# Weight remainders on one engine, and spread bit operations, in a three-part float32 kernel

## The chip, the cores and the metric

The kernel runs on one core of a Trainium2 chip. The metric is the device time of one execution in microseconds (us). The engines are PE (TensorE, matmuls), DVE (VectorE), ACT (ScalarE), POOL (GpSimd) and SP (SyncE, which here only issues transfers).

## What is computed

Three computations stand one behind the other; the last two matter here.

```python
def _attn_ref(q, k, v):        # 4 x 8 heads, 576 positions, 64 wide
    out_d = sm_attn(q_d, k_d, v_d)      # on means of 4 positions
    ...
    return (out_up + out_local)          # plus attention to the 7 nearest

def _moe_ref(x, w_gate, w1, w2):        # 2304 tokens of 512, 8 experts
    expert_idx = np.argmax(logits, axis=1)
    ...
        h = np.maximum(xe @ w1[e], 0.0)  # 512 -> 1024
        ye = h @ w2[e]                   # 1024 -> 512
        out[mask] = gate_w[mask, None] * ye

def _moe2_ref(x, w_in, w_out):          # 512 -> 2048 -> 512
    h = x @ w_in
    g = np.where(pos, h, np.where(neg, 0.0, (h + beta) ** 2 / (4.0 * beta)))
    return (g @ w_out)
```

w_in and w_out arrive as 64-bit floats; everything else is 32-bit.

## The kernel before

Every matmul operand is split into a rounded high part and a remainder, and three products are added: high by high, high by remainder, remainder by high. For a weight the high part (wh) is a cast on ACT (`wconv`, L169) and the remainder (wl) a subtraction (L170), which goes to POOL and DVE in turn. For the hidden tile of an expert the high part (hh) is made on ACT from PSUM (L890) and the remainder (hl) on DVE from PSUM and hh (L891). For an expert's inputs, xh and xl are made likewise from transposes (L893, L894).

The experts run one after another, sorted by their number of tokens, with 416, 360, 336, 312, 300, 288, 272 and 256 columns (CAPS). Expert e has eight steps f, here called slots; g = 8e + f counts them. In slot f TensorE first makes the hidden tile f + 1 (`emit_p1`, L942, twelve matmuls into s) and then takes hidden tile f into the output (`emit_p2`, L956, twelve matmuls into y: eight with hh, then four with hl). In slot 6 and slot 7 the transposes of the next expert's x stand in between, and in slot 7 the next expert's first hidden tile. Behind that, each slot issues weight conversions (`next_wt`: cast, remainder, and the load of the raw weight four places on, wraw, on SP's queue), at most two and only as far as seven buffers allow.

From slot g = CONV0 on, the first eight chunks of the 64-bit weights of the last network are also converted in the expert stage. A chunk goes through four stages: the load (`conv_load`, L815, craw, two buffers); `conv_guard`, a square on ACT (L846) and two operations on POOL (L847, L848); three bit operations on DVE (L834 to L836), which put a 32-bit float together; and the parts, a cast on ACT (L828) and a subtraction on POOL (L829). Each chunk takes four slots, and a chunk's stages lie several slots apart.

All instructions of an engine run in the order in which the code issues them. The rest of the program, the attention ahead of the experts (an order written out as a list) and the last network behind them (L999, L1089), is not touched.

Of the kernel before, what the change touches and what calls it, by code (L numbers as in the profile page):

```python
# [9 lines left out]
F32 = mybir.dt.float32  # L10
# [4 lines left out]
ALU = mybir.AluOpType  # L15
# [9 lines left out]
F2 = 2048  # L25
# [14 lines left out]
NWB, NWC, NWR = 3, 4, 4  # L40
NWT = NWB + NWC
NGR = 4
CONV0 = 16
PAT_MIN = float(np.array(0x38100000, np.uint32).view(np.float32))

C_ID = 0
# [67 lines left out]
def body(ctx: ExitStack, tc: tile.TileContext, qT, kT, kD, vS, vD, wg, w1, w2, w_in, w_out, cst, out, dbg=None, parts="all"):  # L114
    nc = tc.nc
    PE, ACT, DVE, POOL, SP = nc.tensor, nc.scalar, nc.vector, nc.gpsimd, nc.sync
# [11 lines left out]
    def bank(tag):  # L128
        return ps.tile([128, 512], F32, tag=tag, name=tag)
# [27 lines left out]
    wcount = [0]  # L157
# [6 lines left out]
    def wconv(raw):  # L164
        pool = wpools[wcount[0] % len(wpools)]
        wcount[0] += 1
        hi = pool.tile([128, 1024], F32R, tag="wh", name="wh")
        lo = pool.tile([128, 1024], F32R, tag="wl", name="wl")
        ACT.copy(out=hi, in_=raw)  # L169
        (POOL if wcount[0] % 2 else DVE).tensor_tensor(out=lo, in0=raw, in1=hi.bitcast(F32), op=ALU.subtract)  # L170
        return hi, lo

    def w_in_src(w, j):
# [27 lines left out]
    def next_wt():  # L201
        if wpend:
            s, raw = wpend.pop(0)
            wts.setdefault(s, []).append(wconv(raw))
            load_wt()
# [471 lines left out]
    def dve_scale(out, in_, mul):  # L677
# [14 lines left out]
        lo=(lo_, DVE.tensor_copy, ACT.copy), vo=(vo_, dve_scale, act_scale), xm=(xm_, dve_scale, act_scale))  # L692
# [101 lines left out]
    chunks = []  # L794
    for j in range(F2 // 256):
        for c in range(2):
            src = (w_in.bitcast(I32) if wide else w_in)[256 * c:256 * c + 256, :]
            n = 512 if wide else 256
# [4 lines left out]
    cload, cbits, cparts, cdone = [], [], [], [0]  # L803
# [13 lines left out]


    def conv_step():
        if cparts:  # L820
            m = cparts.pop(0)
            r = cdone[0] % 2
            if r == 0:
                pool = wC[cdone[0] // 8 % 2]
                wts.setdefault(E, []).append([pool.tile([128, 1024], F32R, tag=t, name=t) for t in ("wh", "wl")])
            cdone[0] += 1
            hi, lo = (w[:, 512 * r:512 * r + 512] for w in wts[E][-1])
            ACT.copy(out=hi, in_=m)  # L828
            POOL.tensor_tensor(out=lo, in0=m, in1=hi.bitcast(F32), op=ALU.subtract)  # L829
        if cbits:  # L830
            raw, m = cbits.pop(0)
            if wide:
                mi, lo, u = m.bitcast(I32), raw[:, :, 0], raw[:, :, 1]
                DVE.tensor_scalar(out=u, in0=mi, scalar1=3, scalar2=0x3FFFFFFF, op0=ALU.logical_shift_left, op1=ALU.bitwise_and)  # L834
                DVE.scalar_tensor_tensor(out=mi, in0=mi, scalar=-0x40000000, in1=u, op0=ALU.bitwise_and, op1=ALU.bitwise_or)  # L835
                DVE.scalar_tensor_tensor(out=mi, in0=lo, scalar=29, in1=mi, op0=ALU.logical_shift_right, op1=ALU.bitwise_or)  # L836
            cparts.append(m)

    def conv_guard():
        if len(cload) > 1 or cload and len(chunks) in (0, 4 * F2 // 256 - 8):  # L840
            raw = cload.pop(0)
            if wide:
                raw = raw.rearrange("p (x w) -> p x w", w=2)
                hi = raw[:, :, 1].bitcast(F32)
                m = cv.tile([128, 512], F32, tag="cvm", name="cvm")
                ACT.activation(out=m, in_=hi, func=AF.Square)  # L846
                POOL.tensor_scalar(out=m, in0=m, scalar1=PAT_MIN * PAT_MIN, scalar2=None, op0=ALU.is_ge)  # L847
                POOL.tensor_tensor(out=m, in0=hi, in1=m, op=ALU.mult)  # L848
                cbits.append((raw, m))
            else:  # L850
                cbits.append((raw, raw))
# [44 lines left out]
    def xT_parts(sx):  # L896
        s, xr = sx
        cap = CAPS[s]
        parts = x_parts(s)
        r = []  # L900

        def transposes(p_, c, ps_):
            for t, c0, m in ps_:
                PE.transpose(out=p_[:, c0:c0 + m], in_=xr[0:m, t, 128 * c:128 * c + 128], identity=ident[0:m, 0:m])  # L904


        if s == 0:
            first = [next_bank("o") if c < 2 else bank(f"y{c}") for c in range(4)]
            for pt in parts:
                for c in range(4):  # L910
                    transposes(first[c], c, (pt,))
        for c in range(4):
            if s:
                p_ = next_bank("o")
                transposes(p_, c, parts)
            else:
                p_ = first[c]
            hi = mp.tile([128, CAPS[0]], F32R, tag=f"xh{c}", name=f"xh{c}")
            lo = mp.tile([128, CAPS[0]], F32R, tag=f"xl{c}", name=f"xl{c}")
            split_psum(p_[:, 0:cap], cap, False, hi[:, 0:cap], lo[:, 0:cap])  # L920
            r.append((hi, lo))
            if c % 2:
                yield
        yield r
# [9 lines left out]
    def emit_p1(s, f, xhl):  # L934
        cap = CAPS[s]
        h_ps = next_bank("s")
        w = wts[s][2 * (f // 2)]
        n = 0
        for wi, xi in PASSES if f else (PASSES[0], PASSES[2], PASSES[1]):
            for c in range(4):  # L940
                o = 256 * c + 128 * (f % 2)
                PE.matmul(out=h_ps[:, 0:cap], lhsT=w[wi][:, o:o + 128], rhs=xhl[c][xi][:, 0:cap],  # L942
                          start=(n == 0), stop=(n == 11))
                n += 1
        hi = hp.tile([128, CAPS[0]], F32R, tag="hh", name="hh")
        lo = hp.tile([128, CAPS[0]], F32R, tag="hl", name="hl")
        split_psum(h_ps[:, 0:cap], cap, True, hi[:, 0:cap], lo[:, 0:cap])
        return hi, lo
# [12 lines left out]
    def load_off(s):  # L961
        for eng in (ACT, DVE):
            y_off[s, eng] = [eng.value_load(o[0:1, s:s + 1], min_val=0, max_val=NT) for o in (offs_i, loff_i)]
# [39 lines left out]
    def emit_g(h_ps):  # L1003
        r = hp.tile([128, CAP], F32, tag="r", name="r", bufs=2)
        ACT.activation(out=r, in_=h_ps[:, 0:CAP], func=AF.Relu, scale=0.5, bias=half[:, 0:1])  # L1005
        DVE.scalar_tensor_tensor(out=r, in0=r, scalar=1.0, in1=r, op0=ALU.min, op1=ALU.mult)  # L1006
        DVE.tensor_tensor(out=r, in0=h_ps[:, 0:CAP], in1=r, op=ALU.max)  # L1007
        hi = hp.tile([128, CAPS[0]], F32R, tag="hh", name="hh")
        lo = hp.tile([128, CAPS[0]], F32R, tag="hl", name="hl")
        ACT.copy(out=hi[:, 0:CAP], in_=r)  # L1010
        DVE.tensor_tensor(out=lo[:, 0:CAP], in0=r, in1=hi[:, 0:CAP].bitcast(F32), op=ALU.subtract)  # L1011
        return hi, lo
# [11 lines left out]
    for e in range(E):  # L1024
        y_ps = [bank(f"y{c}") for c in range(4)]
        for f in range(8):
            g = 8 * e + f
            if f < 7:
                hln = emit_p1(e, f + 1, xhl)
                if f == 6 and e + 1 < E:  # L1030
                    xTs = xT_parts(sx)
                    next(xTs)
                if f == 3:
                    load_off(e)
                if e + 1 == E and f == 6:
                    gl[0] = emit_g(emit_gmm(0, 0))
                emit_p2(e, f, hl, y_ps)
                if e + 1 == E and f < 4:
                    emit_ysplit(0, f)
            else:  # L1040
                if e + 1 < E:
                    next(xTs)
                emit_p2(e, f, hl, y_ps)
                if e + 1 == E:
                    h_ps = emit_gmm(0, 1)
                emit_y(e, y_ps)
                if e + 1 == E:
                    gl[1] = emit_g(h_ps)
                if e + 1 < E:
                    xhl = next(xTs)  # L1050
                    if e + 2 < E:
                        sx = load_x(e + 2)
                    hln = emit_p1(e + 1, 0, xhl)
            hl = hln
            for _ in range(2):
                if wcount[0] < NWT + g and f != 6:
                    next_wt()
            if 2 <= g < 9:
                emit_places(g - 2)
            if g == 10:  # L1060
                emit_perm()

            if CONV0 <= g:
                if (g - CONV0) % 4 == 0:
                    conv_step()
                    if len(chunks) > 4 * F2 // 256 - 8:
                        conv_load()
                elif (g - CONV0) % 4 == 2:
                    conv_guard()
    while wpend:  # L1070
        next_wt()
    while cload or cbits or cparts:
        conv_step()
        conv_guard()
# [106 lines left out]
```

## Time and profile before

| | |
|---|---|
| time, median of 3 runs | 823.01 us (822.86 to 825.53) |
| the profiled execution | 816.19 us, span 814.4 us |
| PE busy | 763.5 us (94%) |
| DVE busy | 549.5 us (67%) |
| ACT busy | 338.9 us (42%) |
| POOL busy | 347.1 us (43%) |

The span is the time from the first to the last instruction; the execution's own time is 1.8 us longer. Busy time leaves out register and branch work. An engine's share is a mean over the attention (to about 150 us), the experts (to about 402 us) and the last network.

### The profile page before, as it was taken

The page shows a single profiled execution, that of the slowest core. Times are in us where ns is not written, and L with a number is a line of the kernel's source. Part 1 is how long each engine was busy: PE and PEld are TensorE (multiplying, and loading weights), DVE is VectorE, ACT ScalarE, POOL GpSimd, SP SyncE. Part 2 cuts the span into 40 slices and gives each one's busy share as a digit, 9 for nine tenths or more (in the row PEclk, how much of TensorE's full clock was granted, in tenths as well). Part 3 has the DMA queues.
Part 4 walks back from the last instruction along what each step waited for, and adds up shares of the span by engine and source line. Part 5 has one row for each costly group of instructions (what it writes and reads, how often), then busy time and mean ns, then how long its engine had stood idle before and what let it go on. Part 6 is the DMA issues. An engine that isn't in the chain of part 4 may idle for free.

```text
span 814.4 us, 14163 instructions
## 1 busy us (share of the span) xinstructions
PE 763.5 (94%) x5436; PEld 681.5 (84%) x5437; DVE 549.5 (67%) x883; ACT 338.9 (42%) x761; POOL 347.1 (43%) x279
## 2 busy tenths in 40 slices
PE   7658799899999999989999999999999999999995
PEld 3435577599999999879999999999999999999994
DVE  7859878386343877977576677677777777744453
ACT  3637455344344455446254454333333333322221
POOL 3545575352243665773156654233332342221113
PEclk9989879999999999999999999999999999999999
DMA  9997953864455566654301011011011100011112
GB/s 274 243 248 173 236 155 141 262 205 136 149 185 162 181 195 198 189 177 128 103 27 53 27 52 52 27 52 53 27 52 41 39 27 1 0 40 39 39 39 77
DMA packets 51477, 91.71 MB, mean 113 GB/s; under 512 B 3586, under 2 KB 27778, under 8 KB 50734
## 3 DMA queue, kind: packets, MB, share of 16 engines
q1 hardware_dynamic: 46798, 75.13, 31.0%
q0 software_dynamic: 4608, 15.63, 7.1%
q8 instruction: 44, 0.72, 0.4%
q14 instruction: 27, 0.22, 0.1%
HBM read 81.31 MB, written 9.44 MB: 111 GB/s over the span
## 4 chain that ended last, share of the span: by engine, by line
PE 67%; issue 7%; DVE 3%; POOL 2%; ACT 1%; DMA 1%; POOLq 0%; SPq 0%; ACTq 0%
PE s L999 22%; PE y L1089 14%; PE y L956 11%; PE s L942 11%; PE o L1089 7%; PE o L904 1%; POOL out_dram L1104 1%; ACT wh L169 1%; DVE craw L834 1%; DVE wl L170 1%; DVE cvm L835 1%; DMA wraw<-in_dram 1%; DVE hl L891 0%; POOL wl L170 0%; DVE row L859 0%
## 5 line engine op out<-in xcount | busy, mean ns | idle before, releaser
L999 PE MATMUL s<-yT,wh 128*128 128x384 f32 x448 | 141.5, 339 | 0.0
L170 POOL TENSOR_TENSOR wl<-wraw,wh 128x1024 fp32r<-128x1024 f32 x32 | 84.5, 2648 | 101.4 <-ACT wh L169 97.1
L1010 ACT CAST hh<-r 128x384 fp32r<-128x384 f32 x96 | 49.3, 513 | 161.8 <-DVE r L1007 161.8
L1006 DVE SCALAR_TENSOR_TENSOR r<-r 128x384 f32<-128x384 f32 x96 | 61.6, 641 | 67.0 <-ACT r L1005 65.7
L847 POOL TENSOR_SCALAR cvm<-cvm 128x512 f32<-128x512 f32 x32 | 51.0, 1594 | 106.7 <-ACT cvm L846 105.9
L1011 DVE TENSOR_TENSOR hl<-r,hh 128x384 fp32r<-128x384 f32 x96 | 56.9, 592 | 55.7 <-ACT hh L1010 55.1
L1005 ACT ACTIVATE r<-s,half 128x384 f32<-128x384 f32 x96 | 55.8, 581 | 90.2 <-PE s L999 89.8
L999 PEld LDWEIGHTS s<-yT,wh 128*128 128x128 f32 x448 | 83.5, 188 | 4.9
L999 PE MATMUL s<-yh,wh 128*128 128x384 f32 x256 | 85.9, 335 | 0.0
L829 POOL TENSOR_TENSOR wl<-cvm,wh 128x512 fp32r<-128x512 f32 x32 | 49.3, 1540 | 85.0 <-ACT wh L828 73.9
L999 PE MATMUL s<-yh,wl 128*128 128x384 f32 x256 | 85.3, 333 | 0.0
L170 DVE TENSOR_TENSOR wl<-wraw,wh 128x1024 fp32r<-128x1024 f32 x32 | 61.4, 1919 | 23.8 <-ACT wh L169 23.5
L956 PE MATMUL y<-hh,wh 128*128 128x416 f32 (+7 forms) x256 | 76.1, 312 | 0.0
L1089 PE MATMUL y<-wl,hh 128*128 128x512 f32 x192 | 75.7, 394 | 0.0
L1089 PE MATMUL y<-wh,hh 128*128 128x512 f32 x192 | 75.3, 392 | 0.0
L956 PE MATMUL y<-hh,wl 128*128 128x416 f32 (+7 forms) x256 | 74.8, 308 | 0.0
L890 ACT ACTIVATE hh<-s 128x416 fp32r<-128x416 f32 (+7 forms) x64 | 28.0, 437 | 103.8 <-PE s L942 103.8
L169 ACT CAST wh<-wraw 128x1024 fp32r<-128x1024 f32 x64 | 65.7, 1044 | 12.0 <-DMA xs_d<-xr,dst_all 6.4
L1089 PE MATMUL y<-wh,hl 128*128 128x512 f32 x192 | 60.4, 396 | 0.0
L891 DVE SCALAR_TENSOR_TENSOR hl<-s,hh 128x416 fp32r<-128x416 f32 (+7 forms) x64 | 30.7, 482 | 43.6 <-ACT hh L890 43.6
L1007 DVE TENSOR_TENSOR r<-s,r 128x384 f32<-128x384 f32 x96 | 53.5, 557 | 3.3
L956 PE MATMUL y<-hl,wh 128*128 128x416 f32 (+7 forms) x256 | 49.0, 313 | 7.1 <-DVE hl L891 7.0
(276 smaller groups left out, 1769.8 us busy)
## 6 DMA issues: line engine op xcount, KB each, us to landing
wraw<-in_dram SPq DMA_DIRECT2D x88, 512.0 KB, 4.2
v_s<-in_dram SPq DMA_DIRECT2D x12, 512.0 KB, 12.6
kbd<-in_dram SPq DMA_DIRECT2D x24, 200.0 KB, 10.9
xr<-xs_d SPq DMA_DIRECT2D x17, 256.0 KB, 2.8
craw<-in_dram SPq DMA_DIRECT2D x8, 512.0 KB, 3.7
q_t<-in_dram SPq DMA_DIRECT2D x3, 1168.0 KB, 12.5
v_d<-in_dram POOLq DMA_DIRECT2D x6, 288.0 KB, 9.2
k_p<-in_dram POOLq DMA_DIRECT2D x3, 576.0 KB, 7.3
```

The costliest lines, as they stand in the source:

```text
L169: ACT.copy(out=hi, in_=raw)
L170: (POOL if wcount[0] % 2 else DVE).tensor_tensor(out=lo, in0=raw, in1=hi.bitcast(F32), op=ALU.subtract)
L829: POOL.tensor_tensor(out=lo, in0=m, in1=hi.bitcast(F32), op=ALU.subtract)
L847: POOL.tensor_scalar(out=m, in0=m, scalar1=PAT_MIN * PAT_MIN, scalar2=None, op0=ALU.is_ge)
L942: PE.matmul(out=h_ps[:, 0:cap], lhsT=w[wi][:, o:o + 128], rhs=xhl[c][xi][:, 0:cap], start=(n == 0), stop=(n == 11))
L956: PE.matmul(out=y_ps[c][:, 0:cap], lhsT=w[wi][:, o:o + 128], rhs=hl[xi][:, 0:cap], start=(f == 0 and i == 0), stop=(f == 7 and i == 1))
L999: PE.matmul(out=h_ps[:, 0:CAP], lhsT=w[wi][:, o:o + 128], rhs=yhl[j, c][xi], start=(n == 0), stop=(n == 11))
L1005: ACT.activation(out=r, in_=h_ps[:, 0:CAP], func=AF.Relu, scale=0.5, bias=half[:, 0:1])
L1006: DVE.scalar_tensor_tensor(out=r, in0=r, scalar=1.0, in1=r, op0=ALU.min, op1=ALU.mult)
L1007: DVE.tensor_tensor(out=r, in0=h_ps[:, 0:CAP], in1=r, op=ALU.max)
L1011: DVE.tensor_tensor(out=lo[:, 0:CAP], in0=r, in1=hi[:, 0:CAP].bitcast(F32), op=ALU.subtract)
L1089: PE.matmul(out=o_ps[t], lhsT=gl[gi][:, 128 * t:128 * t + 128], rhs=w[wi][:, o:o + 512], start=(f % 4 == 0 and i == 0), stop=(f % 4 == 3 a ...
```

## The change

All weight remainders of the experts go to DVE. The number of conversions in a slot is read from a table, WSTEP, from the second expert on: 2, 1, 2, 1, 1, 1 and none in slots 6 and 7. (The first expert keeps two a slot, and slot 6 is no longer left out there.) The chunks of 64-bit weights start eight slots earlier; the bit operations are issued one in a slot, in the three slots ahead of the parts, and a chunk passes the guard as soon as one is loaded.

```diff
-CONV0 = 16
+CONV0 = 8
+WSTEP = (2, 1, 2, 1, 1, 1, 0, 0)
...
-        (POOL if wcount[0] % 2 else DVE).tensor_tensor(out=lo, in0=raw, in1=hi.bitcast(F32), op=ALU.subtract)
+        DVE.tensor_tensor(out=lo, in0=raw, in1=hi.bitcast(F32), op=ALU.subtract)
...
     def conv_step():
+        conv_parts()
+        for n in range(3):
+            conv_bits(n)
+
+    def conv_parts():
         if cparts:
...
+    def conv_bits(n):
         if cbits:
-            raw, m = cbits.pop(0)
+            raw, m = cbits[0]
             if wide:
                 mi, lo, u = m.bitcast(I32), raw[:, :, 0], raw[:, :, 1]
...
+                if n == 0:
+                    DVE.tensor_scalar(out=u, in0=mi, scalar1=3, scalar2=0x3FFFFFFF, op0=ALU.logical_shift_left, op1=ALU.bitwise_and)
+                elif n == 1:
+                    DVE.scalar_tensor_tensor(out=mi, in0=mi, scalar=-0x40000000, in1=u, op0=ALU.bitwise_and, op1=ALU.bitwise_or)
+                else:
+                    DVE.scalar_tensor_tensor(out=mi, in0=lo, scalar=29, in1=mi, op0=ALU.logical_shift_right, op1=ALU.bitwise_or)
+            if n == 2:
+                cparts.append(cbits.pop(0)[1])
...
-            for _ in range(2):
-                if wcount[0] < NWT + g and f != 6:
+            for _ in range(WSTEP[f] if e else 2):
+                if wcount[0] < NWT + g:
                     next_wt()
...
             if CONV0 <= g:
-                if (g - CONV0) % 4 == 0:
-                    conv_step()
+                r = (g - CONV0) % 4
+                if r == 3:
+                    conv_parts()
                     if len(chunks) > 4 * F2 // 256 - 8:
                         conv_load()
-                elif (g - CONV0) % 4 == 2:
-                    conv_guard()
+                if r < 3:
+                    conv_bits(r)
+                if r == 2:
+                    conv_guard(1)
```

The order of DVE at the switch to the expert of 300 columns, before, from the hl of its first hidden tile to that of its fifth (wl are weight remainders, craw and cvm a chunk's bit operations):

```order
L891 SCALAR_TENSOR_TENSOR hl<-s_4018,hh 128x300
L170 TENSOR_TENSOR wl<-wraw,wh 128x1024
L891 SCALAR_TENSOR_TENSOR hl<-s_4051,hh 128x300
L834 TENSOR_SCALAR craw<-cvm 128x512
L835 SCALAR_TENSOR_TENSOR cvm<-cvm,craw 128x512
L836 SCALAR_TENSOR_TENSOR cvm<-craw,cvm 128x512
L891 SCALAR_TENSOR_TENSOR hl<-s_4093,hh 128x300
L170 TENSOR_TENSOR wl<-wraw,wh 128x1024
L891 SCALAR_TENSOR_TENSOR hl<-s_4128,hh 128x300
L891 SCALAR_TENSOR_TENSOR hl<-s_4167,hh 128x300
```

The same place on DVE of the changed kernel, whose lines are numbered anew (L904 is hl, L171 wl, L844, L846 and L848 the bit operations), between the same two hl:

```order
L904 SCALAR_TENSOR_TENSOR hl<-s_4040,hh 128x300
L904 SCALAR_TENSOR_TENSOR hl<-s_4065,hh 128x300
L171 TENSOR_TENSOR wl<-wraw,wh 128x1024 x2
L844 TENSOR_SCALAR craw<-cvm 128x512
L904 SCALAR_TENSOR_TENSOR hl<-s_4107,hh 128x300
L171 TENSOR_TENSOR wl<-wraw,wh 128x1024
L846 SCALAR_TENSOR_TENSOR cvm<-cvm,craw 128x512
L904 SCALAR_TENSOR_TENSOR hl<-s_4143,hh 128x300
L171 TENSOR_TENSOR wl<-wraw,wh 128x1024 x2
L848 SCALAR_TENSOR_TENSOR cvm<-craw,cvm 128x512
L904 SCALAR_TENSOR_TENSOR hl<-s_4189,hh 128x300
```

No wl stands between the first two hl any more, one bit operation stands where three stood, and five wl lie ahead of the fifth hl where two did.

The order of POOL in the same expert before (the wl of L170 are the experts', the one of L829 a chunk's):

```order
L170 TENSOR_TENSOR wl<-wraw,wh 128x1024 x2
L829 TENSOR_TENSOR wl<-cvm,wh 128x512
L170 TENSOR_TENSOR wl<-wraw,wh 128x1024
L847 TENSOR_SCALAR cvm<-cvm 128x512
L848 TENSOR_TENSOR cvm<-craw,cvm 128x512
```

And in the changed kernel, where L835, L860 and L861 are the former L829, L847 and L848:

```order
L835 TENSOR_TENSOR wl<-cvm,wh 128x512
L860 TENSOR_SCALAR cvm<-cvm 128x512
L861 TENSOR_TENSOR cvm<-craw,cvm 128x512
L835 TENSOR_TENSOR wl<-cvm,wh 128x512
L860 TENSOR_SCALAR cvm<-cvm 128x512
```

The experts' wl are gone from POOL, and the work of the chunks is left. TensorE's order has not changed in any row.

## Rows read from the trace of the kernel before

**Rows 1.** Busy time by stretch; x is instructions, PEclk the granted clock.

```profile
core 0: us, PE busy (x) PEld busy (x) DVE busy (x) ACT busy (x) POOL busy (x), PEclk, DMA share, GB/s
262.00:378.00 116.00, 109.99 (x786) 106.45 (x785) 90.19 (x98) 59.50 (x104) 75.92 (x37) 0.99 0.61 188
...
363.40:366.40 3.00, 2.98 (x13) 2.98 (x14) 1.51 (x2) 0.00 (x0) 2.26 (x2) 0.50 0.27 14
...
402.00:808.00 406.00, 403.19 (x2032) 365.14 (x2030) 272.97 (x422) 147.02 (x282) 143.30 (x122) 1.00 0.11 37
```

**Rows 2.** TensorE in order: start, us, work, idle before it.

```profile
164.65 1.02 PE L942 MATMUL s<-xh,wl 128*128 128x416 f32 x4 [0.27 <-POOL wl L170]
...
204.23 0.93 PE L956 MATMUL y<-hl,wh 128*128 128x360 f32 x4 [0.98 <-DVE hl L891]
...
300.88 0.30 PE L956 MATMUL y<-hh,wh 128*128 128x300 f32 x1
301.02 0.29 PE L956 MATMUL y<-hh,wl 128*128 128x300 f32 x1
302.23 0.82 PE L956 MATMUL y<-hl,wh 128*128 128x300 f32 x4 [0.92 <-DVE hl L891]
302.89 0.72 PE L942 MATMUL s<-xh,wh 128*128 128x300 f32 x4
...
332.18 0.80 PE L956 MATMUL y<-hl,wh 128*128 128x288 f32 x4 [1.36 <-DVE hl L891]
...
357.01 0.66 PE L942 MATMUL s<-xh,wh 128*128 128x272 f32 x4
357.50 0.67 PE L942 MATMUL s<-xl,wh 128*128 128x272 f32 x4
...
359.40 0.29 PE L956 MATMUL y<-hh,wl 128*128 128x272 f32 x1
363.42 1.27 PE L956 MATMUL y<-hl,wh 128*128 128x272 f32 x4 [3.73 <-DVE hl L891]
...
367.02 0.29 PE L956 MATMUL y<-hh,wh 128*128 128x272 f32 x1
```

**Rows 3.** DVE in order, at the switch to the expert of 300 columns.

```profile
294.23 2.59 DVE L170 TENSOR_TENSOR wl<-wraw,wh 128x1024 fp32r<-128x1024 f32 x1 [1.41 <-ACT wh L169]
296.75 0.46 DVE L891 SCALAR_TENSOR_TENSOR hl<-s,hh 128x300 fp32r<-128x300 f32 x1
297.12 2.25 DVE L834 TENSOR_SCALAR craw<-cvm 128x512 int32<-128x512 int32 x1
...
301.71 0.46 DVE L891 SCALAR_TENSOR_TENSOR hl<-s,hh 128x300 fp32r<-128x300 f32 x1
```

**Rows 4.** POOL in order, at the same place.

```profile
293.33 5.76 POOL L170 TENSOR_TENSOR wl<-wraw,wh 128x1024 fp32r<-128x1024 f32 x2 [3.74 <-ACT wh L169]
```

**Rows 5.** Operations on a chunk's tile, 150 to 402 us: duration least/median/longest, ns.

```profile
L846 ACT ACTIVATE cvm<-craw x8: 669/676/682, 256.0 to 359.9; 128x512 f32<-128x512 f32 x8
L847 POOL TENSOR_SCALAR cvm<-cvm x8: 1488/1502/2346, 256.8 to 362.6; 128x512 f32<-128x512 f32 x8
L848 POOL TENSOR_TENSOR cvm<-craw,cvm x8: 1297/1312/1323, 258.4 to 364.4; 128x512 f32<-128x512 f32 x8
L834 DVE TENSOR_SCALAR craw<-cvm x8: 415/2246/2470, 267.5 to 371.0; 128x512 int32<-128x512 int32 x8
...
L836 DVE SCALAR_TENSOR_TENSOR cvm<-craw,cvm x8: 691/1181/2777, 270.5 to 372.2; 128x512 int32<-128x512 int32 x8
...
L829 POOL TENSOR_TENSOR wl<-cvm,wh x8: 1473/1548/1749, 281.5 to 388.8; 128x512 fp32r<-128x512 f32 x8
```

**Rows 6.** Operations on the raw weights, 200 to 402 us, and their loads.

```profile
L169 ACT CAST wh<-wraw x49: 1037/1042/1058, 202.3 to 386.7; 128x1024 fp32r<-128x1024 f32 x49
...
L170 DVE TENSOR_TENSOR wl<-wraw,wh x26: 1207/1671/3062, 198.5 to 390.7; 128x1024 fp32r<-128x1024 f32 x26
...
DMA to landing us min/median/max: 3.4/4.5/6.5
```

More of the change, by code (lines that the diff above doesn't have):

```diff
@@ L829, in conv_step, with conv_guard @@
             POOL.tensor_tensor(out=lo, in0=m, in1=hi.bitcast(F32), op=ALU.subtract)
+    def conv_bits(n):
         if cbits:
-            raw, m = cbits.pop(0)
+            raw, m = cbits[0]
             if wide:
                 mi, lo, u = m.bitcast(I32), raw[:, :, 0], raw[:, :, 1]
[L834 to L840, printed above, removed]
+                if n == 0:
[6 more added lines that the diff above has]
+                cparts.append(cbits.pop(0)[1])
+    def conv_guard(n=2):
+        if len(cload) >= n or cload and len(chunks) in (0, 4 * F2 // 256 - 8):
             raw = cload.pop(0)
```

## The prediction

> **What bounds the kernel now.** I read the page's busy shares first, then the busy time by stretch. From 402 us on, in the second network, TensorE is busy 403.19 of 406 us, and nothing waits in front of it [rows 1]. In the expert stage it is nearly as full, but not quite: from 262 to 378 us it is busy 109.99 of 116 us, while DVE is busy 90.19 and POOL 75.92 [rows 1]. So TensorE bounds both stages, and only its gaps can be won. The change touches no row of TensorE and nothing after 402 us.
>
> The next view was TensorE in order of time, with the reader looking only for the bracket that names an idle time. Between 155 us, where the first expert's matmuls begin, and 402 us there are five: 0.27, 0.98, 0.92, 1.36 and 3.73 us [rows 2]. The first waits for a remainder (wl) that POOL makes, the other four for hl, the remainder of the hidden tile, on DVE.
>
> What each costs is more than its bracket. At 302 us the matmul before the gap starts at 301.02 and the group after the late one at 302.89: 1.87 us for five matmuls that start 0.14 us apart when undisturbed, so 1.17 us are lost, 0.92 of idling and 0.25 of draining and refilling [rows 2]. With 0.25 added to each bracket, the gaps at 164.65, 204.23 and 332.18 us cost 0.52, 1.23 and 1.61 us. The largest has a second bill. From 359.40 to 367.02 us there are 17 starts, which at 0.49 us for four (357.01 to 357.50) would take 2.08 us; they took 7.62, so 5.54 us are lost [rows 2]. The reason that this is so much more than 3.73 is the granted clock: after that gap it is 0.50, the 1.2 GHz level, from 363.4 to 366.4 us, and 1.00 elsewhere [rows 1]. Sum of the five: 0.52 + 1.23 + 1.17 + 1.61 + 5.54 = 10.1 us.
>
> Why hl is late stands in DVE's rows around 300 us. A wl of 2.59 us from 294.23, hl for 0.46, then the three bit operations from 297.12 until the next hl can start at 301.71 [rows 3]. DVE does not work that long; it is held. The same wl takes 1.207 us at its fastest, and L834 and L836 0.415 and 0.691 us, but with medians of 2.246 and 1.181 [rows 5, 6]. POOL meanwhile runs two wl from 293.33 to 299.09 [rows 4]: the DVE wl ends 1.1 us after the first of them, and POOL's two take 5.76 us together with DVE's one in between. DVE's and POOL's instructions with both operands in SBUF take turns, whole instructions at a time. hl, which reads PSUM, runs its 0.46 us in the middle of POOL's second wl [rows 3, 4], so it is held only by what stands ahead of it in DVE's queue.
>
> **The change, part by part.** *Remainders all on DVE.* 32 instructions leave POOL, which took about 2.4 us each (5.76 less 0.96 for DVE's turn, by two) [rows 4], and 32 come to DVE at 1.2 us when not held [rows 6]: 77 us off POOL, 38 us onto DVE. In experts 0 and 1 POOL then has nothing to do, so two wl in a row take DVE 2.4 us, less than one took beside POOL (2.59). The wl awaited at 164.65 us comes 1.2 us earlier, which covers that gap. The gap at 204.23 us has a held wl ahead of its hl, as at 302, and goes too.
>
> The Trainium skill speaks against such a move: "Perfetto Trace Analysis", section "Optimizing Scalar/DVE Operations", says that DVE and GpSimd share an SBUF read port, so that moving work between those two might not help. By that the sum would be nothing; the rows above show the same subtraction at 2.4 us on one and 1.2 on the other, so here the move halves the time for which the others are held.
>
> *No conversions where the next x is split* (WSTEP is 0 for f = 6 and 7). Before, two conversions (f = 7), one with its wl on DVE, stand ahead of the next expert's second hl; now none does, and the eight conversions lie in slots 0 to 5 as 2, 1, 2, 1, 1, 1. TensorE needs a weight two slots or more after that, so no weight comes late. Nothing is added to the queues: the same casts on ACT (1.042 us each) and the same loads on SP, in bunches [rows 6].
>
> *Bits one per step, two experts earlier.* Three operations (0.415 + 0.691 + 0.691 = 1.8 us, the middle one with L836's shape) stood together ahead of one hl; now one stands in each of three slots, in experts 2 to 5. POOL's 1.49, 1.30 and 1.47 us for each chunk stay [rows 5].
>
> *Is anything late next?* I follow the tightest slot, f = 2, in an expert of 288 columns. A matmul there starts about every 0.131 us (between 0.14 at 300 columns and 0.1225 at 272), so twelve take 1.57 and a slot 3.15 us. Zero is the end of the matmuls that feed hl(3). I take 0.45 us for ACT's hh, as for hl. ACT has its two casts done at 1.5 and 2.55 and the square (0.67) at 3.2 [rows 5, 6]. DVE runs wl to 2.7 and to 3.95. POOL's L847, waiting since 3.2, then holds it to 5.45; the last bit operation ends at 6.15, and hl(4) at 6.6. TensorE wants hl(4) after its own slot, two groups of twelve and eight more: 3.15 + 3.15 + 1.05 = 7.35. Slack 0.75 us. In slot 3, L848 to 7.45, wl to 8.65, hl(5) at 9.1 against 10.5. Slack 1.4 us. Slots 0, 1, 4 and 5 have one to three us of it, and at f = 6 the bit operation lies between two pairs of xl that are wanted later still.
>
> Two costs have no row of before, so both ends: if POOL got two turns running, L848's 1.30 us would push hl(4) to 7.9, a loss of 0.55 + 0.25 = 0.8 us in each of four experts. A load issued when slot 0's first wl ends (2.7) feeds the cast due at 6.3 + 1.5 = 7.8; with the median landing of 4.5 us it is there at 7.2, with the longest of 6.5 it is 1.4 us late [rows 6], which costs up to 0.9 us an expert. I take nothing for both, since rows 4 show turns and the median holds; the far end is 3.2 + 3.6 = 6.8 us.
>
> **Sum.** The profiled execution took 816.19 us; less 10.1 that is 806.1. The timed runs have a median of 823.01, 6.8 us more, of which the trace shows nothing; I take the same 10.1 from it: **812.9 us**.
>
> **The rivals.** *Part of it comes back.* The slack of 0.75 us is used up in experts 2 to 5: 3.2 to 3.6 us of gaps, 816.3 us, and with both causes at once 819.7. For it: the slot is the fullest of all. Against: rows 4.
>
> *The waits only move, no gain.* The bits run two experts earlier, and wl and the POOL work of the chunks still take turns; if in experts 2 to 5 one hl each misses by as much as the four did (10.1 over four, 2.5 us each), 823. Against: that needs over 3 us of delay in each, where the largest single hold is 1.5 us. The first rule above, of the Trainium skill's "Perfetto Trace Analysis", would end here too.
>
> *Slower, by one mechanism: DVE becomes the bound.* From 262 to 378 us lie four experts, so 16 moved wl. DVE has 26 us free there [rows 1]. If each still took its held time of 2.59 us [rows 3], that is 41 us, 15 more than there is room, against 9 us won in that stretch or before it: 823 + 15 - 9 = 829. It decides at 26 / 16 = 1.6 us for one wl. For it: the median on DVE is 1.671 [rows 6]. Against: that is beside 76 us of POOL work, of which 38 go.
>
> A rule of the Trainium skill bears on this: "SBUF — State Buffer", section "SBUF: two separate sides", has the pair of ports held for a whole instruction by whichever of DVE and GpSimd starts first, with the other fully blocked. The trace agrees (2.59 us held against 1.207 alone), and what it leaves open is who goes first when both wait.
>
> **How the numbers follow.** Chances: all five gaps gone 0.58, part back 0.24, no gain 0.10, slower 0.08. About 0.3% (2.5 us) is what a measurement here can tell from no change. So faster 0.82, same 0.10, slower 0.08. The range of 809 to 820 us takes in the first two cases and, below, 4 us for the gaps of under 0.2 us that I did not count and for timed runs that may hold longer gaps than the profiled one.
>
> **What the profile after would show.** Right: no wait of TensorE for hl or wl between 155 and 402 us; granted clock 1.00 throughout; the second network starting 10 us earlier; wl on DVE near 1.2 us in experts 0, 1, 6 and 7, up to 2.7 in slots 2 and 3 of the others; L834 at 0.4 and L836 at up to 2.2 us; POOL busy about 77 us less. Wrong: a bracket at the hl pass of slot 4 in experts 2 to 5, an ACT cast that waits for a load, or DVE over 95% busy there.

## The result, and the profile after

The changed kernel takes 811.87 us (median of 16 runs, 803.80 to 817.47) against 820.95 us for the kernel before beside it (16 runs, 815.66 to 827.99): a ratio of 0.9874, with a 95% interval from 0.9843 to 0.9904. (The ratio is reckoned from the fast runs alone, and is not the quotient of the two medians, which is 0.989.) That is 9 to 10 us. The forecast was 812.9 from 823.01, a ratio of 0.9877.

The profiled execution took 814.61 us, its span 812.8 us. These are its waits of TensorE from 155 us to the end of the last network:

```profile
engine line waited for: us in total, times, longest us
PE o L917 <- SPq L709: 1.3, 1, 1.3
PE o L917 <- DMA xr<-xs_d: 0.9, 1, 0.9
```

Both stand ahead of the first expert's matmuls, at the transposes of its x. The five brackets of [rows 2] are gone; no wait for hl or wl is left. Busy time by stretch, the columns as in [rows 1], says the same: TensorE is busy 116.00 of the 116 us from 262 to 378, where it was 109.99, and POOL 31.57 us where it was 75.92. But in the five microseconds where the first expert starts the granted clock is 0.52.

```profile
160.00:165.00 5.00, 4.40 (x16) 3.24 (x17) 1.70 (x4) 2.24 (x5) 0.24 (x1) 0.52 0.81 245
165.00:262.00 97.00, 97.00 (x592) 96.19 (x591) 59.48 (x87) 43.34 (x69) 8.51 (x5) 0.99 0.61 189
262.00:378.00 116.00, 116.00 (x843) 112.48 (x842) 80.77 (x119) 63.28 (x114) 31.57 (x19) 1.00 0.61 193
```

The operations on the raw weights and on a chunk, with least, median and longest duration in ns, answer to [rows 5, 6]. L171 is the weight remainder, L844, L846 and L848 the bit operations:

```profile
L171 DVE TENSOR_TENSOR wl<-wraw,wh x52: 1216/1226/2150, 199.3 to 389.3; 128x1024 fp32r<-128x1024 f32 x52
L844 DVE TENSOR_SCALAR craw<-cvm x8: 416/421/425, 243.6 to 345.7; 128x512 int32<-128x512 int32 x8
L846 DVE SCALAR_TENSOR_TENSOR cvm<-cvm,craw x8: 684/684/689, 246.1 to 348.1; 128x512 int32<-128x512 int32 x8
L848 DVE SCALAR_TENSOR_TENSOR cvm<-craw,cvm x8: 681/890/1101, 251.0 to 350.5; 128x512 int32<-128x512 int32 x8
```

DVE does twice as many remainders, and each takes 1.226 us at the median, where it took 1.671 before. From the first expert's start to the last network DVE executes 229 instructions where it had 198, and is busy for 153.19 us where it was 161.53. L844, once held to 2.246 us, runs in 0.421.

The two spans differ by only 1.6 us, and the reader should not look for the result there. TensorE's order gives better marks: the first matmul of the first expert, of the second expert (360 columns), and of the last network. In the kernel before they start here:

```profile
155.17 1.68 PE L942 MATMUL s<-xh,wh 128*128 128x416 f32 x4 [0.39 <-ACT xh L893]
...
193.91 0.82 PE L942 MATMUL s<-xh,wh 128*128 128x360 f32 x4
...
400.37 0.34 PE L999 MATMUL s<-hi,wh 128*128 128x384 f32 x1
```

And in the changed one:

```profile
163.32 1.94 PE L955 MATMUL s<-xh,wh 128*128 128x416 f32 x4
...
202.65 0.82 PE L955 MATMUL s<-xh,wh 128*128 128x360 f32 x4
...
398.77 0.34 PE L1012 MATMUL s<-hi,wh 128*128 128x384 f32 x1
```

So the attention, which the change does not touch, ended 8.15 us later in this execution; the first expert took 39.33 us instead of 38.74; experts 2 to 8 took 196.12 instead of 206.46, **10.34 us less**; and from there to the end of the span both have 414.03 us.

### The profile page after: what moved, and what is told of

It reads as the page before. It is cut to its first block, busy times and chain, and to the rows that moved or that the text cites. A ratio compares the mean times of both kernels' runs of the same rounds, so it can differ in the third digit from the quotient of the medians.

```text
span 812.8 us, 14123 instructions
## 1 busy us (share of the span) xinstructions
PE 766.1 (94%) x5436; PEld 684.7 (84%) x5437; DVE 545.0 (67%) x915; ACT 339.7 (42%) x761; POOL 265.7 (33%) x247
## 4 chain that ended last, share of the span: by engine, by line
PE 73%; issue 4%; POOL 1%; DVE 0%; ACT 0%; POOLq 0%; ACTq 0%
PE s L1012 22%; PE s L955 14%; PE y L1105 14%; PE y L969 14%; PE o L1105 7%; PE o L917 2%; POOL out_dram L1120 1%; POOLq L1192 0%; POOL gap_t L1122 0%; PE y L917 0%; DVE oacc L1118 0%; ACT r L1018 0%; DVE r L1019 0%; DVE r L1020 0%; DVE hl L1024 0%
## 5 line engine op out<-in xcount | busy, mean ns | idle before, releaser
L860 POOL TENSOR_SCALAR cvm<-cvm 128x512 f32<-128x512 f32 x32 | 52.5, 1640 | 257.2 <-ACT cvm L859 256.8
L171 DVE TENSOR_TENSOR wl<-wraw,wh 128x1024 fp32r<-128x1024 f32 x64 | 81.4, 1292 | 23.7 <-ACT wh L170 23.4
L835 POOL TENSOR_TENSOR wl<-cvm,wh 128x512 fp32r<-128x512 f32 x32 | 50.8, 1586 | 105.7 <-ACT wh L834 94.6
L170 ACT CAST wh<-wraw 128x1024 fp32r<-128x1024 f32 x64 | 65.5, 1047 | 11.9 <-DMA xs_d<-xr,dst_all 6.8
L904 DVE SCALAR_TENSOR_TENSOR hl<-s,hh 128x416 fp32r<-128x416 f32 (+7 forms) x64 | 31.1, 486 | 49.9 <-ACT hh L903 49.7
L1012 PEld LDWEIGHTS s<-yh,wh 128*128 128x128 f32 x256 | 48.0, 188 | 2.7
L955 PE MATMUL s<-xh,wh 128*128 128x416 f32 (+7 forms) x256 | 48.8, 313 | 0.1
```

Source lines behind the costliest of these rows:

```text
L171: DVE.tensor_tensor(out=lo, in0=raw, in1=hi.bitcast(F32), op=ALU.subtract)
L1012: PE.matmul(out=h_ps[:, 0:CAP], lhsT=w[wi][:, o:o + 128], rhs=yhl[j, c][xi], start=(n == 0), stop=(n == 11))
```

## The experiments

Two theories were set against each other. Theory H: POOL's remainders hold DVE, one whole instruction at a time, and so hl is late. Theory O: what counts is the order, that is, how many instructions are issued ahead of hl. The change has three parts that can be made alone: the remainders on DVE, the table WSTEP, and the chunks (earlier, one bit operation a slot). Each of the first six kernels below has one or two of them; the last two add something to the changed kernel. Each kernel was measured beside the kernel before on the same chip, but not all on one chip, so ratios can be compared and times can't. The stages are read as above, from the marks in one profiled execution of each:

| kernel | expert 1, us | experts 2 to 8, us | waits for hl, wl or xl, us | ratio to before (95%) |
|---|---|---|---|---|
| before | 38.74 | 206.46 | 7.3 | 1 |
| changed | 39.33 | 196.12 | 0 | 0.9874 (0.9843 to 0.9904) |
| remainders alone | 40.09 | 196.49 | 0 | 0.9878 (0.9841 to 0.9915) |
| table alone | 40.30 | 219.34 | 16.4 | 1.0189 (1.0150 to 1.0229) |
| chunks alone | 39.36 | 198.90 | 2.1 | 0.9884 (0.9845 to 0.9924) |
| changed without remainders | 40.64 | 197.39 | 0.9 | 0.9842 (0.9806 to 0.9877) |
| changed without table | 39.77 | 196.11 | 0 | 0.9892 (0.9839 to 0.9946) |
| changed without chunks | 39.67 | 197.25 | 0.5 | 0.9897 (0.9847 to 0.9947) |
| changed, POOL busy too | 41.40 | 205.66 | 7.3 | 0.9998 (0.9961 to 1.0035) |
| changed, matmuls between | 38.27 | 196.12 | 0 | 0.9879 (0.9824 to 0.9934) |

From the last network's first matmul to the end of the span every one of them has 414.0 to 414.1 us.

**The remainders alone.** The kernel before with

```diff
-        (POOL if wcount[0] % 2 else DVE).tensor_tensor(out=lo, in0=raw, in1=hi.bitcast(F32), op=ALU.subtract)
+        DVE.tensor_tensor(out=lo, in0=raw, in1=hi.bitcast(F32), op=ALU.subtract)
```

> The kernel before with one part of the change alone: all weight remainders on DVE. The expert stage, from its first matmul to the first of the last network, took 245.2 us before and 235.4 changed. Theory H (POOL's remainders hold DVE, so hl comes late): the gaps are nearly all gone, stage 235 to 237 us, time 9 to 10 us under before. Theory O (what counts is how many instructions are issued ahead of hl: the conversions at the switch of experts and three bit operations together): DVE's queue ahead of hl gets longer, stage 244 us or more, time as before.

No wait is left, and the stage takes 236.58 us: H as forecast, and O is out by 7 us. DVE's queue ahead of hl has become longer, and hl comes in time.

**The table alone.** The kernel before with

```diff
-            for _ in range(2):
-                if wcount[0] < NWT + g and f != 6:
+            for _ in range(WSTEP[f] if e else 2):
+                if wcount[0] < NWT + g:
```

> The kernel before with the table of conversions per slot alone (none in slots 6 and 7). Theory H: POOL's remainders still hold the bit operations and the wl, stage 240 to 244 us. Theory O: half of what stood ahead of hl at the switch is gone, stage about 239 us.

Both theories miss: the stage takes 259.64 us, 14.4 more than before. The gaps at hl come once in each of four experts: 1.33, 4.65, 4.94 and 5.24 us. The second of them is at the switch to the 300 columns, where TensorE's row, DVE's rows and then POOL's read:

```profile
301.39 1.37 PE L969 MATMUL y<-hl,wh 128*128 128x300 f32 x4 [4.65 <-DVE hl L904]
```

```profile
289.45 0.47 DVE L904 SCALAR_TENSOR_TENSOR hl<-s,hh 128x300 fp32r<-128x300 f32 x1 [1.20 <-ACT hh L903]
291.34 2.58 DVE L171 TENSOR_TENSOR wl<-wraw,wh 128x1024 fp32r<-128x1024 f32 x1 [1.42 <-ACT wh L170]
293.85 1.52 DVE L844 TENSOR_SCALAR craw<-cvm 128x512 int32<-128x512 int32 x1
295.40 2.75 DVE L846 SCALAR_TENSOR_TENSOR cvm<-cvm,craw 128x512 int32<-128x512 int32 x1
298.19 2.77 DVE L848 SCALAR_TENSOR_TENSOR cvm<-craw,cvm 128x512 int32<-128x512 int32 x1
300.88 0.83 DVE L904 SCALAR_TENSOR_TENSOR hl<-s,hh 128x300 fp32r<-128x300 f32 x2
```

```profile
290.44 2.41 POOL L171 TENSOR_TENSOR wl<-wraw,wh 128x1024 fp32r<-128x1024 f32 x1 [5.41 <-ACT wh L170]
292.80 2.28 POOL L835 TENSOR_TENSOR wl<-cvm,wh 128x512 fp32r<-128x512 f32 x1
295.05 2.56 POOL L171 TENSOR_TENSOR wl<-wraw,wh 128x1024 fp32r<-128x1024 f32 x1
298.07 2.34 POOL L171 TENSOR_TENSOR wl<-wraw,wh 128x1024 fp32r<-128x1024 f32 x1 [0.46 <-ACT wh L170]
```

Four DVE instructions that take 1.2 + 0.4 + 0.7 + 0.7 = 3.0 us alone lie behind one another, and each waits for one of POOL's: 9.6 us. With the conversions taken out of slot 7, wl, L835 and the three bit operations all fall into slots 0 and 1. So the mechanism is H's, but the order decides how many turns of POOL one hl has to sit through. Neither forecast had put the two together. One wait is gone here, though, the one at the switch to 360 columns (0.98 us before): that is the place for which slot 7 had been emptied.

**The chunks alone**, with CONV0 = 8, `conv_bits` one a slot and `conv_guard(1)` as in the change:

> The kernel before with the chunks alone changed: started eight slots earlier, one bit operation a slot. Theory H: one held operation instead of three stands ahead of hl, but the wl are held still, stage 239 to 243 us. Theory O: stage 237 to 239 us, since the three together were most of the queue at the three largest gaps.

The stage takes 238.26 us, O's figure and just under H's range, with three waits left: 0.26 us for a wl of POOL's, 0.99 at the switch to 360 columns, where no chunk is at work yet, and 0.81 in slot 3 of the expert with 288. In these rows one held bit operation ahead of hl costs little; three in a row, as before and with the table alone, do harm.

**The changed kernel without the remainders on DVE** (that line as before):

> The changed kernel with every second remainder back on POOL. Theory H: gaps of 0.5 to 1.5 us come back in experts 2 to 5, stage 238 to 242 us. Theory O: the order is what counts, stage 235.4 to 236 us and the time as changed.

238.03 us, and waits of 0.24, 0.15 and 0.53 us: H's range at its lower end, with smaller waits than it gave, the first of them in expert 1 and not where H had put them. O, whose stage was 236 us at most, is short by 2 us. In time it was not slower than the changed kernel, so both were run again side by side, at the end of this section.

**The changed kernel without the table**, that is, with `range(2)` and `f != 6`:

> The changed kernel with the old places of the conversions (two in slot 7, none in slot 6). The expert stage took 235.4 us changed, 236.6 with the remainders on DVE alone (no wait of TensorE), 238.3 with the chunks alone, and 259.6 with the table alone. Theory H (POOL's remainders hold DVE instruction by instruction): with them gone the places of the conversions don't matter, no wait, stage 235 to 237 us. Theory O (the order ahead of hl counts too): 0.5 us or more of waits at the switches.

No wait for hl or wl, experts 2 to 8 in 196.11 us against 196.12. The table is worth nothing once the remainders are on DVE. (While POOL has its half, it is worth 1.5 us beside the chunks: 197.39 against 198.90.)

**The changed kernel without the chunks' part** (CONV0 = 16, three together):

> The changed kernel with the chunks as before: sixteen slots late, three bit operations together. Table and chunks alone gave 16.2 us of idle TensorE with the remainders shared; here they are on DVE. Theory H: no wait, or under 0.5 us in all, stage 235 to 237.5 us, since nothing but the chunks' own POOL work holds the three. Theory O: the three in slot 0 behind two wl keep gaps, 2 to 8 us of waits.

236.92 us and one wait of 0.53 us, of transposes for a bank that DVE's xl had not yet freed: H, whose bound was 0.5 us. The chunks' part is worth 1.1 us here (197.25 against 196.12).

**POOL busy too.** DVE keeps all its work; POOL makes every second remainder again into a tile that nobody reads, until six chunks are done (at 324 us):

```diff
         DVE.tensor_tensor(out=lo, in0=raw, in1=hi.bitcast(F32), op=ALU.subtract)
+        if wcount[0] % 2 and cdone[0] < 6:
+            if not spare:
+                spare.append(wC[0].tile([128, 1024], F32R, tag="wl", name="spare"))
+            POOL.tensor_tensor(out=spare[0], in0=raw, in1=hi.bitcast(F32), op=ALU.subtract)
```

> The changed kernel, with POOL making every second remainder once more into a spare tile that nobody reads, up to expert 5: DVE's order is the changed one and no engine but POOL has more to do. Theory H: the wl on DVE take 2.4 us or more again where POOL works beside them, hl comes late in experts 2 to 4, and 4 to 12 us of waits come back, stage 240 to 248 us. Theory O: POOL is not waited for, stage 235 to 236.5 us.

The time is back where it was before the change: 0.9998. The stage takes 247.06 us, and TensorE's waits from the first expert to the last network are

```profile
PE y L974 <- DVE hl L909: 7.0, 10, 1.2
PE o L922 <- DVE xl L912: 0.3, 1, 0.3
```

with these durations (L849 is the first bit operation, L176 POOL's extra work):

```profile
L172 DVE TENSOR_TENSOR wl<-wraw,wh x64: 1208/1225/3427, 152.7 to 396.4; 128x1024 fp32r<-128x1024 f32 x64
L176 POOL TENSOR_TENSOR spare<-wraw,wh x22: 2406/3346/3466, 153.6 to 323.9; 128x1024 fp32r<-128x1024 f32 x22
L849 DVE TENSOR_SCALAR craw<-cvm x8: 420/2622/2632, 243.3 to 352.7; 128x512 int32<-128x512 int32 x8
```

Nobody reads what the 22 added instructions write, and DVE's order is the changed kernel's. They hold DVE's operations, and they are held by them (3.346 us at the median, 2.406 at the least). DVE alone, from the first expert's start to the last network, in the changed kernel and then in this one:

```profile
core 0: us, DVE busy (x), PEclk, DMA share, GB/s
163.32:398.77 235.45, 153.19 (x229) 0.99 0.59 184
...
158.74:405.80 247.06, 191.71 (x229) 0.99 0.56 175
```

The same 229 instructions are busy for 38.5 us more. There is a rival cause: the added instructions also read wraw and wh, so those tiles come free later. SyncE's loads wait for them for 22.3 us in eleven waits, and ACT's casts for 1.5 us in two. But DVE's remainders do not wait longer for their casts (14.9 us in all, 23.4 in the changed kernel), so that is not what makes hl late. All ten waits for hl lie between 191 and 322 us, and the last added instruction starts at 323.9.

That shows that POOL's SBUF work brings the waits back while DVE's order stays as it is. It does not show that the order has no weight: here DVE does all 64 remainders beside a busy POOL, and with half of them moved back to POOL, in the same order, only 0.9 us of waits returned. Nor was it to be expected that the time would come out at that of the kernel before; this is chance.

**Matmuls between the transposes.** In the changed kernel the first matmuls of the first expert run at 1.2 GHz, half of the full clock (0.52 over the five microseconds above). Here three matmuls are put behind each group of transposes:

```diff
             for pt in parts:
                 for c in range(4):
                     transposes(first[c], c, (pt,))
+                w_ps = bank("s0")
+                for _ in range(3):
+                    PE.matmul(out=w_ps, lhsT=onesb, rhs=onesb.unsqueeze(1).to_broadcast([128, 4, 128]), start=True, stop=True)
```

> The changed kernel with three matmuls on ones behind each of the four groups of transposes of the first expert's x. In the changed kernel's trace TensorE waits there 0.88 and 1.35 us for x, the granted clock is 0.52 from 160 to 165 us, and the first twelve expert matmuls take 4.1 us where they took 3.0 at full clock before. If the idling in front is the cause, the clock stays at 1.00 there and the stage takes 234 to 234.8 us; the twelve matmuls cost up to 2.6 us where x is there already, so the time is from 1 us under to 1.5 us over the changed kernel's. If not, the stage stays at 235.4.

The same five microseconds, which in the changed kernel stood at 0.52, now read

```profile
160.00:165.00 5.00, 5.00 (x27) 3.29 (x26) 2.62 (x5) 2.67 (x5) 0.23 (x1) 1.00 1.00 327
```

and the stage takes 234.39 us, 1.06 less. In time nothing of that can be told: 0.9879 beside 0.9874.

**The changed kernel, and the one without its DVE part, on one chip:**

> The changed kernel once more, beside the one without its DVE part on the same chip. From the lengths of the expert stage (235.4 against 238.0 us) the changed kernel should be 2 to 3 us the faster; from the times of different calls (0.9874 against 0.9842 of before) it should be 2 to 3 us the slower. The stage should take 235 to 236.5 us again, with no wait of TensorE between the first expert's start and the last network.

> The changed kernel with every second remainder on POOL, once more. If the stage is what the time follows, the stage takes 237 to 239 us with 0.5 to 1.5 us of waits, and the time is 1.5 to 3.5 us over the changed kernel's of the same call. If the earlier time is right, it is under it.

The stages came out as before, 235.38 and 237.45 us. The medians are 806.36 us (800.98 to 807.67) and 806.27 us (801.26 to 812.56), ratios of 0.9836 (0.9796 to 0.9876) and 0.9858 (0.9808 to 0.9907). The 2 us between the stages are below what six runs each can show, and the earlier lead of the kernel without the DVE part did not repeat. No version was found that beats the changed kernel beyond doubt.

## Why the prediction was right, point by point

**The gaps and their sum.** Right. 10.1 us were forecast, 9.55 of them in experts 2 to 8, where 10.34 were won; TensorE idles nowhere there now. Set start against start, the two traces have won 1.24, 1.20, 1.65 and 5.48 us at the four gaps (9.57), where 1.23, 1.17, 1.61 and 5.54 were forecast. The 0.8 us beyond it were lost where no bracket stands, and the forecast had left such places out. The largest is 0.35 us in the expert of 256 columns, where before these two started 0.36 us apart, and the matmuls ahead of them 0.12:

```profile
386.61 0.28 PE L956 MATMUL y<-hh,wl 128*128 128x256 f32 x1
386.97 0.74 PE L956 MATMUL y<-hl,wh 128*128 128x256 f32 x4
```

In the first expert the gap of 0.52 us went as forecast, too, and yet that expert is 0.59 us longer: its first twelve matmuls took 4.14 us (163.32 to 167.46) where they had taken 3.01 (155.17 to 158.18). "Granted clock 1.00 throughout" was wrong there. It is the profiled execution of before that is the exception: of the twelve executions, two ran these matmuls in 3.0 us, that one and the one with matmuls between the transposes, and the ten others took 3.6 to 4.5. So idling ahead of them is the likely cause. That the ratio was met to 0.0003 is partly luck, since the uncounted 0.8 us and this 1.1 us work against each other, and the interval reaches ten times as far to either side.

**The mechanism.** Right. With POOL's remainders moved and nothing else, the waits go (206.46 to 196.49 us); with POOL kept busy beside the changed order of DVE, they return. But it is one way to the gain and not the only one: the chunks' part and the table win 9.1 us together while POOL keeps its half (206.46 to 197.39), by leaving fewer held instructions ahead of one hl. One reading of the rows was too narrow: the turns were put down to instructions "with both operands in SBUF", but L834 reads one tensor and was held too, 2.25 us in [rows 3] against 0.415 at its fastest. The 0.96 us taken off for DVE's turn stands in no row; the 2.4 us that came of it is right, for POOL's remainders before took 2.343 us at the least and 2.410 at the median (200 to 402 us). The Trainium skill's sentence in "Perfetto Trace Analysis", section "Optimizing Scalar/DVE Operations", that moving work between DVE and GpSimd might not help, was outweighed as forecast: moving it to the faster of the two gave 0.9878.

**The parts.** Here the text claimed too much. The step "No conversions where the next x is split" counted the emptied slot 7 as a help ahead of the second hl. It does remove the wait there (the one at 360 columns is gone in the kernel with the table alone), but that kernel is 12.9 us slower in experts 2 to 8, since the conversions then fall into the slots of the bit operations; and within the change the table is worth nothing. Of the other two parts the remainders alone give nearly all (10.0 us of the 10.3) and the chunks alone three quarters (7.6). They don't add up, because both work on the same waits: the remainders cure all four, the chunks alone leave the one at 360 columns and a shorter one in the expert of 288.

**The tightest slot.** Its slack of 0.75 us was mis-sized, on the safe side. In the expert of 288 columns the rows of the changed kernel, DVE's and then POOL's, are

```profile
337.36 2.36 DVE L171 TENSOR_TENSOR wl<-wraw,wh 128x1024 fp32r<-128x1024 f32 x2 [0.48 <-ACT wh L170]
339.64 1.10 DVE L848 SCALAR_TENSOR_TENSOR cvm<-craw,cvm 128x512 int32<-128x512 int32 x1
340.66 0.45 DVE L904 SCALAR_TENSOR_TENSOR hl<-s,hh 128x288 fp32r<-128x288 f32 x1
341.40 2.15 DVE L171 TENSOR_TENSOR wl<-wraw,wh 128x1024 fp32r<-128x1024 f32 x1 [0.30 <-ACT wh L170]
```

```profile
338.93 2.14 POOL L860 TENSOR_SCALAR cvm<-cvm 128x512 f32<-128x512 f32 x1 [8.62 <-ACT cvm L859]
341.15 1.32 POOL L861 TENSOR_TENSOR cvm<-craw,cvm 128x512 f32<-128x512 f32 x1
```

The forecast had hl(4) wait for all of the former L847. L848 took 1.10 us beside it, 0.41 over its 0.69 alone, instead of the 2.2 reckoned. hl(4) was done at 341.11 and its first matmul ran at

```profile
343.19 0.69 PE L969 MATMUL y<-hl,wh 128*128 128x288 f32 x4
```

so the slack is 2.1 us. L861 held the next wl by 0.9 us, as forecast, and neither far end (two turns running, a late load) came about: wl's longest is 2.150 us, and in the experts no cast on ACT is put down as waiting for a load.

**The base.** The 6.8 us between the profiled execution and the median of before were left as unknown. The marks of the twelve profiled executions tell where such differences lie. In the two of the changed kernel the first expert's first matmul starts at 163.32 and 152.60 us, while experts 2 to 8 agree to 0.02 us and the last network to 0.1. Over all twelve that start lies between 148.0 and 163.3 us. So what varies most from one execution to the next is the attention stage, not the stage of the change, which is why the same 10 us could be taken from either number. The forecast sign of this, "the second network starting 10 us earlier", fell to it: 1.6 us in this pair of executions, 9.75 counted from the first expert's start.

**The rivals.** None came true. "DVE becomes the bound" fails by its own figure, 1.6 us for one wl: the median is 1.226. Its sum has a slip: all five gaps lie before 378 us, so 10.1 us and not 9 come off, and 828 us would follow. No gain is what the kernel with a busy POOL shows (0.9998), and the table alone shows that one of the three parts can make it slower (1.0189).

## What to carry to other kernels

Where DVE and POOL both work from SBUF, count turns, not busy time: each DVE instruction may have to sit through one of POOL's (here four of 3.0 us took 9.6), so a wait grows with the number of short DVE instructions ahead of the one that TensorE needs. Work that takes POOL 2.4 us and DVE 1.2 cost DVE less here when DVE did it all. Two cures can be in a bundle, and also a part that cures nothing or does harm; making and undoing one part at a time shows which is which.

## What was not expected of the hardware

L860, a POOL instruction with one tensor operand, held a DVE instruction with two by 0.41 us, while L861 and the remainders, with two operands, held such ones to their end. Whether the operand is the reason was not tried. And TensorE's clock at the start of the experts is not the same in every execution: with waits of 1.08, 0.73 and 0.39 us ahead of the first expert's matmuls the kernel before kept the granted clock at 1.00, with waits of 0.88 and 1.35 us the changed one started at the 1.2 GHz level, 1.1 us the longer for its first twelve matmuls. The sum of the waits does not decide it: the kernel with the chunks alone had 0.88, 0.70 and 0.43 us, less than before, and took 3.64 us for the twelve. What does is open.
